# One order of 815 operations exchanged for another in a fused SSM and long-convolution kernel

## The chip, the cores and the metric

The kernel runs on one core of a Trainium2 chip. A core has five engines that run their own instruction queues side by side: TensorE (PE; its weight loads are shown apart, as PEld), VectorE (DVE), ScalarE (ACT), GpSimd (POOL) and SyncE (SP), which here only issues DMAs. They wait for each other by semaphores. PE writes its results into PSUM, which this kernel uses as 8 banks; DVE and ACT carry ("evict") them from there to SBUF. The metric is the device time of one execution in microseconds, the median of several runs.

## The reference

Two layers work on sequences of 2048 steps and 640 features; their outputs are put side by side. Setup and types are left out.

```python
def _A_ref(x, Lambda_re, Lambda_im, B_re, B_im, C_re, C_im, log_dt, Dskip):
    Lam_bar = exp(exp(log_dt) * Lam)
    B_bar = ((Lam_bar - 1.0) / Lam)[:, None] * Bmat
    Bu = einsum("bld,pd->blp", x, B_bar)
    for t in range(L):
        h = Lam_bar * h + Bu[:, t]          # 640 complex states
    return 2.0 * einsum("blp,dp->bld", hseq, Cmat).real + x * Dskip
...
def _B_ref(q, k, v, shift_k, ssm_k, ssm_D):
    k_shift = sum(k_pad[:, t:t + S] * shift_k[:, 3 - t] for t in range(4))
    kv = k_shift * v
    y = irfft(rfft(kv, 2 * S) * rfft(ssm_k, 2 * S))[:S]
    return q * (y + kv * ssm_D)
...
concatenate([a, b], axis=-1)
```

## The kernel before, in words

**One table sets everything.** The program is written as 815 operations. An operation is one step such as "these 20 matmuls" or "evict this PSUM group", with the memory that it reads and writes, from which its dependencies are found. A string, `ORDER` (behind line 1115), lists all of them: each entry has the operation's number, a letter for its engine (A = ACT, V = DVE, G = POOL, T = PE, t = PE in a narrow form of 64 output columns, S = SP) and a digit for its first PSUM bank. Line 1175 or so turns the string into a list, and `Program.emit` walks through it: each engine gets its operations in this order and runs them in this order, whatever else is ready. An operation waits for its dependencies, and the first one of a PSUM group also for the last holder of its banks. So the order decides what is queued behind a waiting instruction, the bank digit decides whose eviction a matmul waits for, and the letter decides what an eviction costs. Some operations have no instructions with some engines: where ACT evicts a group (a plain copy), a following operation multiplies or adds on DVE or POOL; where DVE evicts, it does both in one instruction, and the follower is empty.

**Part A (the SSM).** x is loaded transposed (L547), B_bar is built from the parameters (L517 and L512 load, L524 turns it). The base matmuls (L581) form Bu for blocks of 16 steps. Going up, neighbours are joined by multiplying with tables of powers of Lam_bar (four large tables, L457, multiplied on PE at L602; a fifth instruction at L457 is for part B); the groups are evicted at L598, L622 and L648. C is transformed with PE at L571 (evicted at L575). A scan over the 128 blocks (L679 to L690, all on DVE) reads its swapped input from a PSUM group at L679. Going down, L225 or L229 are the matmuls (a wide and a narrow form) and L728 (DVE) or L726 (ACT) the additions; the innermost level comes last. Sixteen output tiles follow: x is loaded (L736) into one of four buffers, multiplied with Dskip (L737; Dskip is loaded at L372), 20 matmuls (L225 or, narrow, 40 at L229), eviction on DVE (L754) or on ACT (L752) with an addition (L760) on POOL, and a store (L765). A load at L736 thus waits for the store, four tiles earlier, that read its buffer.

**Part B (the convolution).** k and v are loaded transposed (L814) in five slices, each convolved with four taps (products at L205 on DVE or L206 on ACT, sums at L840) and multiplied with v (L841), then written to DRAM (L847) and read back in another layout (L857). The transform goes in two stages per half of the features: L876 or L881 with evictions at L886, L900 with evictions at L913, both for the kernel ssm_k (loaded at L807) and for kv. The products in the frequency domain are five instructions per quarter (L924, two L927, L929, L931). Back it goes by L951 (evicted at L956) and L972, evicted on ACT (L988, then L995 multiplies with q) or on DVE (L990, with q at once); q is loaded at L825 in four pieces per half, and stored at L1006.

The names in the rows: `arena` is all of SBUF, `acc` all of PSUM, `kv_rows` the DRAM scratch.

## Time and profile before

| what | us |
|---|---|
| median of 3 runs | 188.28 (188.27 to 188.59) |
| span of the profiled execution | 187.3 |
| around the span, against that median | 0.98 |
| PE busy | 175.6 |
| DVE busy | 158.0 |
| ACT busy | 147.7 |
| POOL busy | 72.6 |

The profiled execution has no time of its own beside its span; the median of the runs stands in for it. A span is counted from the first to the last instruction on the engines. Busy times of one engine's instructions overlap slightly, since the next one starts before the last has left the pipeline. In all rows, an arrow in brackets names what ended the idle time before an instruction, and times are microseconds.

### The profile page before, as it was taken

How to read it: one execution, taken by the hardware profiler on the slowest of the kernel's cores; microseconds unless marked ns; L12 is line 12 of the kernel's file. 1: busy time of each engine (PE TensorE's matmuls, PEld its weight loads, DVE VectorE, ACT ScalarE, POOL GpSimd, SP SyncE). 2: the span in 40 equal slices, each digit the busy share in tenths (PEclk: the TensorE clock that was granted, in tenths of full speed). 3: DMA queues.
4: the chain of work that ended last, by engine and by line, in shares of the span. 5: the costliest groups of instructions: out<-in, count | busy, mean ns of one | idle time of the engine just before them, and what ended most of it. 6: DMA issues, size and time to landing. Idle time of an engine off the chain costs nothing.

```text
span 187.3 us, 7665 instructions
## 1 busy us (share of the span) xinstructions
PE 175.6 (94%) x3398; PEld 126.3 (67%) x3399; DVE 158.0 (84%) x225; ACT 147.7 (79%) x181; POOL 72.6 (39%) x68
## 2 busy tenths in 40 slices
PE   7998999999799979979997999999999999999992
PEld 2565666677468756656685688776588876887770
DVE  3537964679959899999969999899999999998961
ACT  2469699989899979999997997997898883985000
POOL 8679999900000000008803925730740000551620
PEclk9999999999999999999999999999999999999999
DMA  5999999799999989999989479402496993058996
GB/s 153 191 184 158 200 143 140 141 174 182 198 253 154 290 179 152 180 182 154 138 109 251 154 170 133 75 5 72 122 196 120 210 227 85 15 160 187 208 219 173
DMA packets 106682, 30.15 MB, mean 161 GB/s; under 512 B 101274, under 2 KB 106010, under 8 KB 106650
## 3 DMA queue, kind: packets, MB, share of 16 engines
q1 hardware_dynamic: 106332, 29.35, 86.7%
q8 instruction: 26, 0.43, 1.1%
q10 hardware_dynamic: 318, 0.33, 0.6%
q14 instruction: 6, 0.05, 0.1%
HBM read 11.32 MB, written 7.86 MB: 102 GB/s over the span
## 4 chain that ended last, share of the span: by engine, by line
PE 54%; DVE 23%; DMA 9%; ACT 8%; issue 3%; DVEq 0%; ACTq 0%
PE acc L225 17%; PE acc L581 13%; DMA arena<-in_B_k_dram 9%; PE acc L229 6%; DVE arena L728 6%; PE acc L900 6%; DVE arena L205 5%; ACT arena L913 5%; PE acc L951 4%; DVE arena L840 3%; PE acc L972 3%; PE acc L539 2%; DVE arena L754 2%; PE acc L881 1%; ACT arena L886 1%
## 5 line engine op out<-in xcount | busy, mean ns | idle before, releaser
L581 PE MATMUL acc<-arena 128*64 128x512 bf16 x400 | 45.6, 380 | 1.8 <-DVE arena L457 1.1
L913 ACT CAST arena<-acc 128x960 bf16<-128x960 f32 (+1 forms) x43 | 37.4, 916 | 4.0 <-PE acc L900 2.2
L225 PE MATMUL acc<-arena 128*128 128x320 bf16 (+2 forms) x255 | 36.4, 297 | 2.2 <-DVE arena L754 1.1
L581 PEld LDWEIGHTS <-arena 128*64 128x64 bf16 x400 | 26.0, 110 | 17.8 <-DVE arena L457 1.3
L886 ACT CAST arena<-acc 128x1024 bf16<-128x1024 f32 x37 | 35.8, 1034 | 2.1 <-PE acc L881 2.0
L225 PEld LDWEIGHTS <-arena 128*128 128x128 bf16 x256 | 23.7, 98 | 12.1 <-DVE arena L754 1.3
L841 POOL TENSOR_TENSOR arena<-arena 128x2048 bf16<-128x2048 bf16 x2 | 8.8, 4410 | 53.7 <-DVE arena L840 46.1
L900 PE MATMUL acc<-arena 128*64 128x160 bf16 x512 | 23.6, 235 | 1.8 <-DVE arena L679 1.4
L900 PEld LDWEIGHTS <-arena 128*64 128x64 bf16 x512 | 18.6, 110 | 8.3 <-ACT arena L913 2.2
L229 PE MATMUL acc<-arena 128*64 128x320 bf16 (+3 forms) x258 | 23.2, 313 | 0.5 <-DVE arena L690 0.5
L840 DVE TENSOR_TENSOR arena<-arena 128x2048 bf16<-128x2048 bf16 x14 | 17.6, 1256 | 4.5 <-ACT arena L206 4.3
L728 DVE TENSOR_TENSOR arena<-acc,arena 128x1024 bf16<-128x1024 f32 (+2 forms) x19 | 20.4, 1114 | 0.9 <-PE acc L229 0.5
L760 POOL TENSOR_TENSOR arena<-arena 128x640 bf16<-128x640 f32 x3 | 4.2, 1416 | 32.6 <-ACT arena L752 32.6
L956 ACT CAST arena<-acc 128x1024 bf16<-128x1024 f32 x16 | 15.4, 1025 | 1.7 <-PE acc L951 1.6
L229 PEld LDWEIGHTS <-arena 128*64 128x64 bf16 x258 | 13.0, 110 | 3.5 <-DVE arena L690 0.6
L876 PE MATMUL acc<-arena 128*64 128x128 bf16 x400 | 14.6, 220 | 0.2 <-ACT arena L886 0.2
L876 PEld LDWEIGHTS <-arena 128*64 128x64 bf16 x400 | 12.9, 110 | 2.4 <-ACT arena L886 0.9
L205 DVE TENSOR_SCALAR arena<-arena 128x2048 bf16<-128x2048 bf16 x15 | 11.0, 749 | 3.6 <-DMA arena<-in_B_k_dram 3.5
L754 DVE TENSOR_TENSOR arena<-acc,arena 128x640 bf16<-128x640 f32 x13 | 10.7, 820 | 3.5 <-PE acc L225 2.2
L206 ACT ACTIVATE arena<-arena 128x2048 bf16<-128x2048 bf16 (+2 forms) x10 | 11.1, 1112 | 1.5 <-DMA arena<-in_B_k_dram 1.5
L924 DVE TENSOR_TENSOR arena<-arena 128x2560 bf16<-128x2560 bf16 x8 | 11.9, 1484 | 0.1
L602 PE MATMUL acc<-arena 128*64 128x256 bf16 (+2 forms) x140 | 11.6, 291 | 0.1
(142 smaller groups left out, 284.4 us busy)
## 6 DMA issues: line engine op xcount, KB each, us to landing
out_dram<-arena SPq DMA_DIRECT2D x32, 160.0 KB, 3.3
arena<-in_B_ssm_k_dram SPq DMA_DIRECT2D x8, 320.0 KB, 6.1
kv_rows<-arena SPq DMA_DIRECT2D x5, 512.0 KB, 4.7
arena<-kv_rows SPq DMA_DIRECT2D x16, 160.0 KB, 4.0
arena<-in_A_x_dram SPq DMA_DIRECT2D x16, 160.0 KB, 3.5
arena<-in_B_q_dram SPq DMA_DIRECT2D x8, 320.0 KB, 6.3
arena<-in_A_B_im_dram ACTq DMA_DIRECT2D x1, 160.0 KB, 2.8
arena<-in_A_B_re_dram SPq DMA_DIRECT2D x1, 160.0 KB, 3.0
```

The lines of the kernel that those rows point to most:

```text
L205: vm = lambda e: lambda out, in_, by: e.tensor_scalar_mul(out=out, in0=in_, scalar1=by)
L225: e.matmul(out, lhsT=lhsT, rhs=rhs, start=start, stop=stop, skip_group_check=True)
L229: e.matmul(out[half], lhsT=lhsT[:, half], rhs=rhs, start=start, stop=stop, skip_group_check=True, tile_position=(0, 64 * r))
L581: e.matmul(o[64 * r:64 * r + 64], lhsT=self.BT[j][:, r, d, :], rhs=self.XP[:, d, 2 * q:2 * q + 2], start=(d == 0), stop=(d == 4), skip_gro ...
L728: e.tensor_tensor(out=o, in0=b, in1=o, op=ALU.add)
L754: e.tensor_tensor(out=two(ys), in0=two(B)[:, :, 0:320], in1=two(ys), op=ALU.add)
L840: P.add(f"ca{d}_{j}", tt, lambda e: e.tensor_tensor(out=t1, in0=t1, in1=t2, op=ALU.add), outs=[t1], ins=[t1, t2])
L876: e.matmul(B[64 * b:64 * b + 64, 128 * i:128 * i + 128], lhsT=lh[i], rhs=F[:, b, :], start=True, stop=True, tile_position=(0, 64 * b))
L886: P.add(f"e1{what}{hf}_{u}", {PACT: act(1024), PDVE: dve(1024)}, lambda e, B: c.CP[e](out=out, in_=(B.rearrange("p (l n s k) -> p k s l n" ...
L900: e.matmul(B[64 * s:64 * s + 64, 512 * b + 160 * i:512 * b + 160 * i + 160], lhsT=c.W[:, k, 64 * b:64 * b + 64], rhs=self.AS[hf][:, k, 160 ...
L913: c.CP[e](out=out, in_=b.rearrange("p r (k j n) -> p r k j n", k=n, j=4) if nj > 1 else b.rearrange("p r (k x) -> p r k x", k=n))
L956: P.add(f"er2{hf}_{u}", {PACT: act(1024), PDVE: dve(1024)}, lambda e, B: c.CP[e](out=out, in_=B.rearrange("p (s n b) -> p b s n", s=2, n=4 ...
```

## The change

Only the string changes. All operations and their dependencies stay, and all entries stand in another order. 57 operations change their engine, 8 matmul groups their form (the number of matmuls goes from 3399 to 3395), and 309 of the 418 operations that belong to a PSUM group get another bank.

```diff
 ORDER = (
-    "67G0 22V0 4T0 25V0 171T1 26G0 23V0 65V0 148G0 39V0 66V0 112G0 59V0 72G0 9T0 183S0 165T2 46G0 30G0 169T0 69G0 180S0 92T3 "
...
+    "148G0 18V0 125V0 19V0 65V0 23V0 20V0 13V0 182S0 9T4 39V0 66V0 69G0 92T5 8T6 93V5 171T7 94A0 95V0 37V0 72G0 122V0 10T0 102V0 22V0 "
...
```

From ACT to DVE go 19 operations: five evictions of part A's upward levels and of B_bar, five of L886 and L913, three conv taps, two small scalings, three evictions at L956 and L990, and the eviction of output tile 10 (L752 before, L754 now). From DVE to ACT go eleven: two upward evictions, two at L575, one L886, one small L728, three L956, one L990 and the eviction of output tile 15. From DVE to POOL go the one L457 of part B, an L929, an L931, four L737 and some followers; from POOL to DVE two L927, three L737 and some followers. Some loads change the queue between SP and ACT.

**First place: DVE around the fourth k slice.** The two L205 of the double row multiply the fourth k slice, as soon as it has landed, with its first two taps; L679, L682, L683 and L684 are the scan of part A's first half; the L457 ahead is part B's. Before:

```order
L666 COPY arena<-arena 128x1280
L841 TENSOR_TENSOR arena<-arena 128x2048
L457 TENSOR_TENSOR arena<-arena 128x1280
L682 TENSOR_TENSOR arena<-arena 128x640
L668 MEMSET arena 128x10
L205 TENSOR_SCALAR arena<-arena 128x2048 x2
L679 TENSOR_TENSOR arena<-acc,arena 128x640
L840 TENSOR_TENSOR arena<-arena 128x2048
L683 TENSOR_TENSOR arena<-arena 128x640
L205 TENSOR_SCALAR arena<-arena 128x2048
```

Now:

```order
L841 TENSOR_TENSOR arena<-arena 128x2048
L913 CAST arena<-acc 128x2x3x4x40
L679 TENSOR_TENSOR arena<-acc,arena 128x640
L682 TENSOR_TENSOR arena<-arena 128x640
L668 MEMSET arena 128x10
L683 TENSOR_TENSOR arena<-arena 128x640
L205 TENSOR_SCALAR arena<-arena 128x2048 x2
L684 SCALAR_TENSOR_TENSOR arena<-arena 128x640
L840 TENSOR_TENSOR arena<-arena 128x2048
L205 TENSOR_SCALAR arena<-arena 128x2048
```

L679, which stood behind the double L205, stands ahead of it, as do L682 and L683; in front of L679 there is now an eviction (L913). The L457 has gone to POOL. Further up, of part A's four tables (L457, numbers 0 to 3) before made 0 and 3 early, and 1 and 2 between the conv instructions of the second k slice. Now 0 and 1 come early, ahead of every conv instruction, and 2 and 3 as a double row directly ahead of the third k slice's first two L205.

**Second place: SP around the load of Dskip.** L814 are the transposing loads of k and v, L807 those of ssm_k's second half. Before:

```order
L814 DMA_TRANSPOSE arena<-in_B_v_dram 128x2048
L736 DMA arena<-in_A_x_dram 128x640
L814 DMA_TRANSPOSE arena<-in_B_k_dram 128x2048
L556 DMA_TRANSPOSE arena<-in_A_C_re_dram 128x1x640
L736 DMA arena<-in_A_x_dram 128x640
L807 DMA arena<-in_B_ssm_k_dram 32x80x64 x4
L372 DMA arena<-in_A_Dskip_dram 128x640
L736 DMA arena<-in_A_x_dram 128x640
```

Now:

```order
L814 DMA_TRANSPOSE arena<-in_B_v_dram 128x2048
L556 DMA_TRANSPOSE arena<-in_A_C_re_dram 128x1x640
L372 DMA arena<-in_A_Dskip_dram 128x640
L814 DMA_TRANSPOSE arena<-in_B_k_dram 128x2048
L807 DMA arena<-in_B_ssm_k_dram 32x80x64 x4
L736 DMA arena<-in_A_x_dram 128x640 x2
L814 DMA_TRANSPOSE arena<-in_B_v_dram 128x2048
```

The load of Dskip (L372), which stood behind the fifth k slice and four ssm_k pieces, stands ahead of both.

**Third place: SP around the last load of q.** L765 stores output tiles of part A, L736 loads an x tile into the buffer of such a store, L1006 stores part B. Before:

```order
L765 DMA out_dram<-arena 128x640
L825 DMA arena<-in_B_q_dram 32x32x160
L736 DMA arena<-in_A_x_dram 128x640
L825 DMA arena<-in_B_q_dram 32x32x160
L736 DMA arena<-in_A_x_dram 128x640
L765 DMA out_dram<-arena 128x640 x3
L736 DMA arena<-in_A_x_dram 128x640 x3
L1006 DMA out_dram<-arena 32x16x160 x4
```

Now:

```order
L765 DMA out_dram<-arena 128x640
L736 DMA arena<-in_A_x_dram 128x640
L765 DMA out_dram<-arena 128x640 x3
L736 DMA arena<-in_A_x_dram 128x640
L825 DMA arena<-in_B_q_dram 32x32x160
L736 DMA arena<-in_A_x_dram 128x640
L1006 DMA out_dram<-arena 32x16x160
L736 DMA arena<-in_A_x_dram 128x640
```

The last piece of q (L825) for the second half stood ahead of the three stores of tiles 9, 11 and 10; it now stands behind the three, which are in the order 10, 9, 11, and behind the L736 that loads into the buffer of tile 10.

**On PE**, at the last L728 of the innermost level, an L951 group of the first half now stands ahead of the L900 that needs the freed bank, where before it stood behind the output tile that follows. In the second half, an L951 group stands ahead of an L972 that it used to follow.

76 rows, old and new, of the table ORDER are left out of this document.

## The prediction

> **What bounds the kernel now.** I read the page first, for span and engine shares; then busy time by stage; then the chain of waits; then who waits for whom on TensorE (PE) and VectorE (DVE); last the timelines around the longest waits. The page and the windows:
>
> ```profile
> span 187.3 us, 7665 instructions
> PE 175.6 (94%) x3398; PEld 126.3 (67%) x3399; DVE 158.0 (84%) x225; ACT 147.7 (79%) x181; POOL 72.6 (39%) x68
> ...
> core 0: us, PE busy (x) PEld busy (x) DVE busy (x) ACT busy (x) POOL busy (x), PEclk, DMA share, GB/s
> 0.00:40.00 40.00, 38.37 (x343) 23.53 (x345) 25.18 (x69) 30.80 (x38) 34.03 (x51) 1.00 1.05 166
> 40.00:60.00 20.00, 18.76 (x301) 13.32 (x298) 16.89 (x23) 18.34 (x27) 0.00 (x0) 1.00 1.11 189
> 60.00:141.00 81.00, 76.04 (x1731) 56.23 (x1730) 76.94 (x89) 74.67 (x92) 28.76 (x11) 1.00 0.84 152
> 141.00:187.30 46.30, 42.38 (x1034) 33.18 (x1029) 39.01 (x47) 23.84 (x27) 9.79 (x6) 1.00 0.73 160
> ```
>
> The mean share of PE hides three regimes. Up to 40 us PE works on the base matmuls, DVE is loose and POOL builds tables. From 60 to 141 us DVE is busy 76.94 of 81.00 us and ACT 74.67: there is no room on either, and PE waits for them in small pieces. After 141 us ACT is half idle. The chain of waits shows which of these times counts (start, length, what):
>
> ```profile
> 41.15 1.42 DVE arena L205 x2
> ...
> 46.67 0.98 DVE arena L457
> ...
> 65.20 1.42 DVE arena L205 x2
> 66.62 0.74 DVE arena L679
> 67.41 0.61 PE acc L900 x12
> ...
> 135.91 1.24 DVE arena L728
> 137.19 1.93 PE acc L900 x48
> ...
> 161.68 5.47 PE acc L951 x160
> ...
> 169.98 1.70 PE acc L972 x176
> ```
>
> So there are two gates on DVE. **Gate 1** is the last L728 (the innermost level of A's downward scan), which ends at 135.91 + 1.24 = 137.15: it frees the PSUM bank that the next L900 needs, and from there PE runs on almost without a gap. **Gate 2** is the last product of part B, which ends at 159.82 + 1.68 = 161.5 and lets the second inverse stage (L951) begin:
>
> ```profile
> 159.82 1.68 DVE L931 TENSOR_TENSOR arena<-arena 128x1280 bf16<-128x1280 bf16 x2
> ```
>
> Between 41.15, where DVE gets the second k tile, and gate 1 lie 96.0 us that DVE must fill; its waits there are few:
>
> ```profile
> DVE arena L205 <- DMA arena<-in_B_k_dram: 3.5, 3, 1.9
> DVE arena L737 <- DMA arena<-in_A_Dskip_dram: 1.4, 1, 1.4
> ...
> 53.96 0.75 DVE L205 TENSOR_SCALAR arena<-arena 128x2048 bf16<-128x2048 bf16 x1 [1.90 <-DMA arena<-in_B_k_dram]
> ...
> 65.20 1.42 DVE L205 TENSOR_SCALAR arena<-arena 128x2048 bf16<-128x2048 bf16 x2 [0.65 <-DMA arena<-in_B_k_dram]
> ...
> 97.87 0.49 DVE L737 TENSOR_TENSOR arena<-arena 128x640 bf16<-128x640 bf16 x1 [1.38 <-DMA arena<-in_A_Dskip_dram]
> ```
>
> And two waits of PE for DVE are single long ones, both early:
>
> ```profile
> 48.12 2.35 PE L581 MATMUL acc<-arena 128*64 128x512 bf16 x20 [1.15 <-DVE arena L457]
> ...
> 67.41 0.61 PE L900 MATMUL acc<-arena 128*64 128x160 bf16 x12 [1.39 <-DVE arena L679]
> ```
>
> **The sum** is made against the profiled execution: span 187.3 us. The median of the runs shown is 188.28, that is 0.98 us around the span, which I keep.
>
> **What goes.** (1) Of the four tables at L457, before makes numbers 0 and 3 early and 1 and 2 between the conv instructions (L205, L840) of the second k slice, and PE waits 1.15 us for number 1. In the new order 0 and 1 come early, and 2 and 3 stand as a pair where DVE waited 1.90 us for the third k slice: the wait of PE goes, and that of DVE is filled. (2) L679 stood behind two L205 that wait for the fourth k slice; it now stands ahead of them, so the 1.39 us of PE go and the 0.65 us of DVE are covered by L679 and its neighbours. (3) The Dskip load stood in SP's queue behind big loads; it now stands ahead of the fifth k slice and of four ssm_k loads, and the 1.38 us should go. For DVE that is 1.90 + 0.65 + 1.38 = 3.93 us of waits.
>
> A new wait comes: the eviction L913 that stands just ahead of L679 waits for its matmuls on PE. No row shows it. Its bounds: nothing, if PE is ahead, up to the 1.39 us for which PE stood at that place; less than nothing is excluded, since a wait saves no work. I take 0.8, near the middle, since the wait and PE's own are two sides of one late pair.
>
> **What comes.** DVE gets more to do, by these groups of the page and of the view by shape:
>
> ```profile
> L886 DVE CAST arena<-acc 128x1024 bf16<-128x1024 f32 x3 | 3.6, 1215 | 0.0
> L913 DVE CAST arena<-acc 128x960 bf16<-128x960 f32 x3 | 3.5, 1154 | 0.0
> L927 DVE TENSOR_TENSOR arena<-arena 128x1280 bf16<-128x1280 bf16 x14 | 11.4, 819 | 0.1
> L929 POOL TENSOR_TENSOR arena<-arena 128x1280 bf16<-128x1280 bf16 x1 | 2.6, 2617 | 0.1
> L737 DVE TENSOR_TENSOR arena<-arena 128x640 bf16<-128x640 bf16 x11 | 7.4, 686 | 1.4 <-DMA arena<-in_A_Dskip_dram 1.4
> L575 DVE CAST arena<-acc 128x640 bf16<-128x640 f32 x4 | 3.3, 815 | 0.0
> L457 DVE TENSOR_TENSOR arena<-arena 128x1280 bf16<-128x1280 bf16 x5 | 8.2, 1652 | 0.0
> ```
>
> From 41.15 to the last product, DVE gains one L886 (1.22), three L913 (3.46), two L927 (1.64), two L737 (1.37) and small ones (one conv tap and one L648, together 1.2; three tiny scalings 0.4), 9.3 in all. It loses one L457 that goes to POOL (1.65), two L575 to ACT (1.63), an L929 and an L931 to POOL (1.64, at the 0.82 of an L927), three L737 (2.06, one of them only passes behind the last product) and small ones (0.9), 7.9 in all. Net **+1.4**. But the L931 and two of the lost L737 stood behind gate 1, so there these 2.2 us count as no loss, and DVE has 1.4 + 2.2, some 3.5 us, more to do ahead of it. Neighbouring DVE rows overlap (the chain counts 0.74 of an L679 that lasts 0.82), so 3.5 of durations are about 3.2 of time, and 1.4 are 1.3.
>
> Gate 1: +3.2 − 3.93 + 0.8 = **+0.1**. Unchanged, then; but one L951 group (16 of the 160 matmuls that last 5.47 us in the chain, 0.5 us) is now issued ahead of the L900 that waits there, so PE has 0.5 less left behind it: **−0.4** on the end.
> Gate 2: +1.3 − 3.93 + 0.8 = −1.8 if DVE alone set it. It can't get all of that, since the products take evictions of matmuls that come behind gate 1, and these come only 0.4 earlier. Ends −0.4 and −1.8; I take the middle, −1.1. An L972 group of 48 matmuls now stands behind this gate, where it stood ahead (48 of the 176 that last 1.70, so +0.4): **−0.7**.
>
> The later of the two decides, and they differ by less than I know them: I take **−0.6**. At the start, loads and weights trade places on SP and ACT's queue. PE's base matmuls run 38.37 of 40.00 us there, so a shift of a load can cost or bring up to the 1.63 that is left; I take nothing, for want of a row that leans either way. Evictions that pass from ACT to DVE cost a fifth more each (1215 ns against 1034):
>
> ```profile
> L886 ACT CAST arena<-acc 128x1024 bf16<-128x1024 f32 x37 | 35.8, 1034 | 2.1 <-PE acc L881 2.0
> ```
>
> That is inside the count above; what ACT is relieved of buys time only where ACT was late. Eight matmul groups change form: 4 instructions fewer, the L229 forms take about 0.3 us each: nothing.
>
> **A rule that speaks against it.** POOL gets the L457, an L929 and an L931 while DVE is full. Do they hinder each other? The trace has rows for both sides (duration in ns: least, median, most):
>
> ```profile
> L457 DVE TENSOR_TENSOR arena<-arena x5: 1481/1483/2326, 18.7 to 62.6; 128x1280 bf16<-128x1280 bf16 x5
> ...
> L737 DVE TENSOR_TENSOR arena<-arena x11: 481/484/1685, 97.9 to 175.0; 128x640 bf16<-128x640 bf16 x11
> ...
> 84.01 4.08 POOL L841 TENSOR_TENSOR arena<-arena 128x2048 bf16<-128x2048 bf16 x1 [46.12 <-DVE arena L840]
> 101.44 4.74 POOL L841 TENSOR_TENSOR arena<-arena 128x2048 bf16<-128x2048 bf16 x1 [7.61 <-DMA arena<-in_B_v_dram]
> ```
>
> So yes: now and then an instruction of DVE is longer by 0.84 or 1.20 us, or one of POOL by 0.66. The Trainium skill, page "SBUF — State Buffer", section "Who interferes with whom", has the reason: a DVE instruction with two SBUF inputs and a GpSimd instruction that reads SBUF share one port pair, and the one that comes second is blocked entirely. By that rule each POOL instruction added beside a full DVE may cost up to its own length, and one more of 2.6 us would make the sum +2.0 instead of −0.6. The trace agrees in kind, but the losses that it shows are fractions of a POOL instruction. My own count goes by the rows: in exchange for the three above and two L737, POOL gives up two L927 and two L737, one instruction more net; I count it at nothing, and one encounter more costs 0.84.
>
> **The rivals.**
> *The waits gone count in full.* DVE's extra work falls into gaps, both gates move by the waits alone, and PE gains 1.15 + 1.39: the end comes 1.8 (gate 2's lower end) to 2.5 earlier. Time about 186.3. For it: the chain does run through both waits. Against it: 76.94 busy of 81.00.
> *Nothing moves, or what is won is given back.* PE has 42.38 of 46.30 us behind 141 and the gates stay; or one more encounter of POOL and DVE takes 0.84 of the 0.6 won. Time 188.1 to 188.5. That the change doesn't do what it says is excluded as far as order goes: engines run their rows in order. But (3) may only hand the wait to the k load that Dskip now precedes.
> *DVE is overfull (slower).* The 3.2 us ahead of gate 1 aren't covered, because the waits of the three k loads are set by the transposes and recur at later instructions: then the gate moves +3.2 less a part, +1 to +2.5. Time 189.3 to 190.8.
> *The last q load comes late (slower).* This is the one I fear most. All L988 and L990 of the second half need four q loads (L825). Before, the last was issued long before its use:
>
> ```profile
> 150.62 1.27 SPq L825 DMA_DIRECT2D arena<-in_B_q_dram  x1
> ...
> SPq L736 <- DMA out_dram<-arena: 7.0, 5, 2.3
> ...
> L825 SPq DMA_DIRECT2D arena<-in_B_q_dram x8: 400/605/1693, 134.8 to 150.6; - x8
> ...
> DMA to landing us min/median/max: 4.2/6.3/7.6
> ```
>
> Now it stands on SP behind three stores of A's tiles and a load (L736) that waits until the first of these stores has landed. That store's tile is evicted on DVE behind all products, at about 161; it is waited for at most 2.3 us (the longest of the five waits above), then the load is issued, and q follows at about 164. Landing after 4.2 is 168.2, after the median 6.3 it is 170.3, after 7.6 171.6. In the chain of before the L972 ahead of these evictions begin at 169.98, and 176 of their matmuls last 1.70; in the new order 160 (1.55) precede the L225 that needs the bank of the first eviction, so with 0.6 won PE is there at 170.9. An eviction of 1.15 (as L913) stands between: PE stalls by what the landing exceeds 169.8, that is 0 to 1.8 us. Time 187.7 to 189.5, more if the issue itself slips. The deciding point is the landing at 169.8. Against it: fewer loads are under way then than at 144, so the landing should be nearer to 4.2 than to 7.6.
>
> **How the numbers follow.** The runs differ by 0.2% (188.27 to 188.59), about what a measurement of this kernel can tell from no change: faster means below 187.90, slower above 188.66. The forecast, −0.2 to −1.2 around **187.7**, gets 0.38; waits in full 0.10; nothing moves 0.21; DVE overfull 0.13; late q 0.18, of which 0.01 still ends faster and 0.01 within 0.2%. Of the forecast 0.02 falls within 0.2%. Faster 0.36 + 0.10 + 0.01 = 0.47, same 0.21 + 0.02 + 0.01 = 0.24, slower 0.13 + 0.16 = 0.29. The range leaves out the better half of the full waits and the worst of the two slower cases: 186.2 to 190.0. The forecast's own range is 187.1 to 188.1.
>
> **What would show it.** Right: no PE wait on L457 or L679 at 45 to 70 us over 0.5; no L737 wait on Dskip; the last L728 ending within 0.7 us of 137.15, the last L931 at about 160.4. Late q: a PE wait at an L225 near 171 on an L988 or L990, with L825 landing behind 169.8. Overfull: the last L728 ends behind 138. Wrong altogether: a wait of over 1 us at a place that none of these names, above all at the start, where the forecast has only a bound.

## The result, and the profile after

| what | before | after |
|---|---|---|
| median of the runs, one chip | 188.34 (188.27 to 188.59) | 196.25 (195.25 to 197.74) |
| ratio | | 1.0424 [1.0373, 1.0474] |
| span of the profiled execution | 187.3 | 194.6 |
| PE / DVE / ACT / POOL busy | 175.6 / 158.0 / 147.7 / 72.6 | 177.5 / 164.4 / 139.4 / 77.6 |

The change makes the kernel slower by 4.2%, some 8 us. Times and ratios here and below are those of the fast executions: one that took over 1.5% longer than the fastest of its kernel is left out. The profiled execution of after has a time of its own, 196.35, so 1.75 us lie around its span.

The page of after, and its busy time in the stretches that the prediction used (the last one ends later now):

```profile
span 194.6 us, 7661 instructions
...
PE 177.5 (91%) x3395; PEld 126.5 (65%) x3395; DVE 164.4 (85%) x231; ACT 139.4 (72%) x173; POOL 77.6 (40%) x70
...
0.00:40.00 40.00, 36.70 (x331) 21.55 (x333) 29.10 (x76) 24.70 (x34) 35.83 (x51) 1.00 1.09 165
40.00:60.00 20.00, 19.76 (x320) 13.28 (x317) 18.20 (x20) 17.56 (x22) 0.57 (x1) 1.00 1.10 218
60.00:141.00 81.00, 73.78 (x1644) 54.55 (x1640) 75.48 (x89) 69.21 (x89) 29.28 (x11) 0.98 0.88 145
141.00:194.60 53.60, 47.25 (x1116) 37.09 (x1112) 41.66 (x49) 27.90 (x32) 11.96 (x9) 0.99 0.63 140
```

Up to 40 us PE does 1.7 us less than before, and from 40 to 60 a full us more. Between 60 and 141 us it loses 2.3 us of busy time and 87 matmuls, and the granted clock is no longer 1.00. The waits say on whom (total, times, longest):

```profile
PE acc L900 <- DVE arena L728: 4.0, 3, 3.3
PE acc L581 <- DMA arena<-in_A_B_re_dram: 2.0, 1, 2.0
...
PE acc L225 <- ACT arena L988: 0.9, 1, 0.9
...
DVE arena L205 <- DMA arena<-in_B_k_dram: 3.2, 1, 3.2
...
ACT arena L988 <- DMA arena<-in_B_q_dram: 3.0, 1, 3.0
```

The waits on L457, L679 and Dskip are gone. In their place stands one long one: DVE waits 3.2 us for the fifth k slice, and PE 3.3 us for the L728 behind it. The timelines of DVE and PE show both, one behind the other:

```profile
90.80 1.42 DVE L205 TENSOR_SCALAR arena<-arena 128x2048 bf16<-128x2048 bf16 x2 [3.16 <-DMA arena<-in_B_k_dram]
92.14 3.81 DVE L728 TENSOR_TENSOR arena<-acc,arena 128x1024 bf16<-128x1024 f32 x4
96.75 1.16 DVE L913 CAST arena<-acc 128x960 bf16<-128x960 f32 x1 [0.81 <-PE acc L900]
...
93.41 0.61 PE L900 MATMUL acc<-arena 128*64 128x160 bf16 x12 [3.30 <-DVE arena L728]
```

Why does the fifth slice come late? All k slices use one buffer (`KT`; v has three), so a load may be issued only when the last tap has read the slice before it. The timeline of DVE around the third slice, in after:

```profile
48.86 1.23 DVE L841 TENSOR_TENSOR arena<-arena 128x2048 bf16<-128x2048 bf16 x1
50.01 1.22 DVE L886 CAST arena<-acc 128x1024 bf16<-128x1024 f32 x1
52.68 0.83 DVE L666 COPY arena<-arena 128x1280 f32<-128x1280 f32 x1 [1.46 <-PE acc L881]
53.42 2.88 DVE L457 TENSOR_TENSOR arena<-arena 128x1280 bf16<-128x1280 bf16 x2
56.23 1.41 DVE L205 TENSOR_SCALAR arena<-arena 128x2048 bf16<-128x2048 bf16 x2
...
61.18 0.75 DVE L205 TENSOR_SCALAR arena<-arena 128x2048 bf16<-128x2048 bf16 x1
...
63.23 1.23 DVE L841 TENSOR_TENSOR arena<-arena 128x2048 bf16<-128x2048 bf16 x1
64.59 1.16 DVE L913 CAST arena<-acc 128x960 bf16<-128x960 f32 x1
```

With L841 DVE is through with the second slice, at 48.86 + 1.23 = 50.09 (before: 1.90 ahead of 53.96, so 52.06). Yet the third slice's taps start at 56.23, where they started at 53.96 before. In front of them stand not only the two tables, but an eviction (L886) and a copy (L666) that itself waits 1.46 us for PE. The last tap ends at 61.18 + 0.75 = 61.93. SP's issues in the timeline of before, from the fourth k slice to the fifth:

```profile
59.81 3.06 SPq L814 DMA_TRANSPOSE arena<-in_B_k_dram  x1
...
74.64 2.93 SPq L814 DMA_TRANSPOSE arena<-in_B_v_dram  x1
...
78.25 2.16 SPq L814 DMA_TRANSPOSE arena<-in_B_k_dram  x1
```

And in that of after:

```profile
61.96 2.23 SPq L814 DMA_TRANSPOSE arena<-in_B_k_dram  x1
...
77.07 3.34 SPq L814 DMA_TRANSPOSE arena<-in_B_v_dram  x1
80.46 2.05 SPq L556 DMA_TRANSPOSE arena<-in_A_C_re_dram  x1
82.56 0.58 SPq L372 DMA_DIRECT2D arena<-in_A_Dskip_dram  x1
83.24 3.79 SPq L814 DMA_TRANSPOSE arena<-in_B_k_dram  x1
```

The fourth slice's load goes out 0.03 us behind that tap, 2.15 us later than before; in a_r16k4, below, it also follows by 0.03. SP issues one load after the other, and v comes 2.4 us late too. Then C and Dskip, which stand ahead of the fifth k slice now, take 2.8 us more, and that slice is issued 5.0 us later than before.

The end of after, by its chain of waits (start, length, what), shows the last q load:

```profile
167.84 3.52 DMA out_dram<-arena
...
171.75 5.40 DMA arena<-in_B_q_dram
...
177.26 0.70 ACT arena L988
...
178.00 5.61 PE acc L225 x40
```

It is issued behind the store that L736 waits for, lands at 177.15, and the eviction behind it holds PE for 0.9 us.

### The profile page after: what moved, and what is told of

Same layout as the page of the kernel before. It is cut to its first block, busy times and chain, and to the rows that moved or that the text cites. A ratio compares the mean times of both kernels' runs of the same rounds, so it can differ in the third digit from the quotient of the medians.

```text
span 194.6 us, 7661 instructions
## 1 busy us (share of the span) xinstructions
PE 177.5 (91%) x3395; PEld 126.5 (65%) x3395; DVE 164.4 (85%) x231; ACT 139.4 (72%) x173; POOL 77.6 (40%) x70
## 4 chain that ended last, share of the span: by engine, by line
PE 39%; DVE 18%; DMA 17%; SPq 12%; ACT 8%; issue 4%; DVEq 0%; ACTq 0%
PE acc L581 16%; PE acc L225 7%; DVE arena L728 5%; PE acc L229 5%; DMA out_dram<-arena 4%; SPq L807 4%; DMA arena<-in_A_B_re_dram 4%; SPq L547 4%; PE acc L602 3%; PE acc L900 3%; DVE arena L754 3%; DMA arena<-in_B_q_dram 3%; PE acc L876 2%; ACT arena L913 2%; DMA arena<-in_B_v_dram 2%
## 5 line engine op out<-in xcount | busy, mean ns | idle before, releaser
L913 ACT CAST arena<-acc 128x960 bf16<-128x960 f32 (+1 forms) x40 | 35.2, 896 | 9.9 <-PE acc L900 9.5
L225 PE MATMUL acc<-arena 128*128 128x320 bf16 (+3 forms) x262 | 38.0, 299 | 1.3 <-ACT arena L988 0.9
L886 ACT CAST arena<-acc 128x1024 bf16<-128x1024 f32 x36 | 34.9, 1032 | 3.3 <-PE acc L876 1.5
L225 PEld LDWEIGHTS <-arena 128*128 128x128 bf16 x262 | 24.2, 98 | 11.2 <-ACT arena L988 1.0
L900 PE MATMUL acc<-arena 128*64 128x160 bf16 x512 | 24.3, 243 | 4.3 <-DVE arena L728 4.0
L900 PEld LDWEIGHTS <-arena 128*64 128x64 bf16 x512 | 20.1, 115 | 9.4 <-DVE arena L728 5.6
L229 PE MATMUL acc<-arena 128*64 128x320 bf16 (+3 forms) x248 | 22.1, 310 | 1.3 <-DVE arena L690 0.6
L728 DVE TENSOR_TENSOR arena<-acc,arena 128x1024 bf16<-128x1024 f32 (+2 forms) x18 | 20.0, 1154 | 0.3 <-PE acc L229 0.2
L841 POOL TENSOR_TENSOR arena<-arena 128x2048 bf16<-128x2048 bf16 x2 | 8.3, 4164 | 26.6 <-DMA arena<-in_B_v_dram 17.5
L205 DVE TENSOR_SCALAR arena<-arena 128x2048 bf16<-128x2048 bf16 (+1 forms) x20 | 14.7, 752 | 3.4 <-DMA arena<-in_B_k_dram 3.2
L956 ACT CAST arena<-acc 128x1024 bf16<-128x1024 f32 x17 | 16.3, 1027 | 1.3 <-PE acc L951 1.3
L754 DVE TENSOR_TENSOR arena<-acc,arena 128x640 bf16<-128x640 f32 x13 | 10.7, 822 | 3.9 <-PE acc L225 2.8
L927 DVE TENSOR_TENSOR arena<-arena 128x1280 bf16<-128x1280 bf16 x16 | 12.6, 819 | 0.2
L309 POOL TENSOR_TENSOR arena<-arena 128x512 int32<-128x512 int32 x8 | 12.3, 1546 | 0.7 <-DVE arena L435 0.6
L457 POOL TENSOR_TENSOR arena<-arena 128x1280 bf16<-128x1280 bf16 x1 | 3.1, 3147 | 22.9 <-ACT arena L648 22.9
```

The source lines that it names most:

```text
L205: vm = lambda e: lambda out, in_, by: e.tensor_scalar_mul(out=out, in0=in_, scalar1=by)
L225: e.matmul(out, lhsT=lhsT, rhs=rhs, start=start, stop=stop, skip_group_check=True)
L229: e.matmul(out[half], lhsT=lhsT[:, half], rhs=rhs, start=start, stop=stop, skip_group_check=True, tile_position=(0, 64 * r))
L728: e.tensor_tensor(out=o, in0=b, in1=o, op=ALU.add)
L754: e.tensor_tensor(out=two(ys), in0=two(B)[:, :, 0:320], in1=two(ys), op=ALU.add)
L886: P.add(f"e1{what}{hf}_{u}", {PACT: act(1024), PDVE: dve(1024)}, lambda e, B: c.CP[e](out=out, in_=(B.rearrange("p (l n s k) -> p k s l n" ...
```

## The experiments

Ratios are against runs of before on the same chip, with their 95% intervals. Before took 186.6 to 187.6 us there.

### Single suspects of after

**a_ctl** is after once more, on another chip: 194.67, ratio 1.0427 [1.0367, 1.0487]. The loss doesn't hang on the chip.

> The changed kernel itself, as the yardstick for the three runs beside it on the same chip: 1.042 times before, within the 1.0373 to 1.0474 measured.

**a_k4tap** moves the fifth slice's load ahead of the fourth v slice's, and, as the one buffer then demands, the fourth slice's last tap forward on DVE:

```diff
 DVE
 L840 TENSOR_TENSOR arena<-arena 128x2048
+L205 TENSOR_SCALAR arena<-arena 128x2048
 L679 TENSOR_TENSOR arena<-acc,arena 128x640
...
 L684 SCALAR_TENSOR_TENSOR arena<-arena 128x640
-L205 TENSOR_SCALAR arena<-arena 128x2048
 SP
+L814 DMA_TRANSPOSE arena<-in_B_k_dram 128x2048
 L814 DMA_TRANSPOSE arena<-in_B_v_dram 128x2048
 L556 DMA_TRANSPOSE arena<-in_A_C_re_dram 128x1x640
 L372 DMA arena<-in_A_Dskip_dram 128x640
-L814 DMA_TRANSPOSE arena<-in_B_k_dram 128x2048
```

> The changed kernel, with the last tap of the fourth k slice (L205) put back on DVE directly behind that slice's third sum, and the load of the fifth k slice (L814) put on SP ahead of the fourth v slice, of C and of Dskip. Theory 'late k slice' (the fifth slice lands at 90.7 instead of 84.2, DVE waits 3.2 us for it and PE 3.3 behind that): the slice lands before 86, both waits go, and the time falls by 3.3 to 4.4 us, to 192.0 to 193.0. Theory 'DVE overfull' (the wait only stands where DVE would be late anyway): it falls by less than 1.5 us, to 195 or more.

Measured: 193.50, ratio 1.0318 [1.0256, 1.0381]. DVE no longer waits for k, and PE's wait falls from 3.30 to 1.72 us, not to nothing: the v slice, later now, brings a POOL product beside the two taps, which take 3.07 us instead of 1.42 (DVE's and POOL's timelines):

```profile
88.07 3.07 DVE L205 TENSOR_SCALAR arena<-arena 128x2048 bf16<-128x2048 bf16 x2
...
85.86 4.07 POOL L841 TENSOR_TENSOR arena<-arena 128x2048 bf16<-128x2048 bf16 x1 [19.32 <-DMA arena<-in_B_v_dram]
```

So the k wait is worth about 1% of the 4.2, by point values whose intervals just overlap.

**a_k4first** puts the fifth slice's load directly behind the fourth v slice, ahead of C and Dskip, and moves nothing on DVE. **a_k4q** does the same and brings the last q load ahead, as a_q below.

```diff
 L814 DMA_TRANSPOSE arena<-in_B_v_dram 128x2048
+L814 DMA_TRANSPOSE arena<-in_B_k_dram 128x2048
 L556 DMA_TRANSPOSE arena<-in_A_C_re_dram 128x1x640
 L372 DMA arena<-in_A_Dskip_dram 128x640
-L814 DMA_TRANSPOSE arena<-in_B_k_dram 128x2048
```

> The changed kernel with the load of the fifth k slice on SP directly behind the fourth v slice, ahead of C and Dskip; nothing else is moved, DVE keeps its order. In the run that put k ahead of v and the tap back, DVE's wait for k was gone, but the two L205 took 3.07 us instead of 1.42, since the v slice came later and POOL's L841 fell beside them. Theory 'late k slice, and the port': here v is not delayed, L841 on POOL is over by 88.3, k lands at about 87, L205 takes 1.4 to 2.0, and 3.0 to 3.6 us are won against the changed kernel. Theory 'DVE overfull': under 1.5.

> The same and also the last load of q ahead of the three stores. Theory 'late q': 0.9 to 1.3 us less than the kernel with the k slice alone. Rival: the same within 0.4.

Measured: 194.07, ratio 1.0389 [1.0329, 1.0449], and 193.30, 1.0350 [1.0293, 1.0406]. The k wait is gone, but now C is late, and PE waits for it (a_k4first):

```profile
PE acc L571 <- DMA arena<-in_A_C_re_dram: 2.2, 1, 2.2
```

What stands in this queue is a closed sum: with everything 2.2 us late, one load or another is waited for, whichever comes last.

**a_start** gives the start loads before's order. It came out at 204.12, ratio 1.0865 [1.0797, 1.0932], and tells nothing of the start: the load of shift_k fell behind the transposes, and its cast on ACT, with the evictions behind it, waited 9.45 us.

> The changed kernel with the loads at the start (B, parameters, x, B transposed, shift_k, first k slice) in the order and on the queues of before. Theory 'start': the second B transpose lands at 18.5 instead of 19.9, the base matmuls go on 1.3 us earlier, and this stays to the end: about 195.0. Rival 'absorbed': at 60 us the changed kernel's PE has the same lost time as before's (the lag of 1.35 is made up by then), so the k slices and DVE set the time from there and the end moves by less than 0.4: 195.9 to 196.3.

**a_start2** avoids that: shift_k's load goes behind the B transposes, and its cast (L796) behind the evictions on ACT.

```diff
 SP
-L547 DMA_TRANSPOSE arena<-in_A_x_dram 128x5x256 x2
-L790 DMA arena<-in_B_shift_k_dram 128x5x4
-L547 DMA_TRANSPOSE arena<-in_A_x_dram 128x5x256 x2
+L547 DMA_TRANSPOSE arena<-in_A_x_dram 128x5x256 x4
 L512 DMA_TRANSPOSE arena<-in_A_B_im_dram 128x5x384
 L512 DMA_TRANSPOSE arena<-in_A_B_re_dram 128x5x384
+L790 DMA arena<-in_B_shift_k_dram 128x5x4
```

> The changed kernel with the load of shift_k behind the two B transposes on SP, as before had it, and the small cast that reads it (L796, on ACT) moved to just ahead of the first tap, since it made all of ACT wait for this load in the first try. Theory 'start': the second B transpose lands 0.6 to 1.4 earlier and the end comes as much earlier. Rival 'absorbed': the end moves by less than 0.4, because the k slices and DVE set the pace from 45 us on.

Measured: 194.14, ratio 1.0410 [1.0334, 1.0486] beside 1.0427 for a_ctl. PE's wait for B is 0.8 us; with after's start it is 2.0 in after and 1.1 in a_ctl, so the edit takes away 0.3 to 1.2. The end shows nothing of it that can be told from noise, and the intervals are too wide to exclude such an amount.

**a_q** issues the last q load ahead of the three stores:

```diff
 L736 DMA arena<-in_A_x_dram 128x640
+L825 DMA arena<-in_B_q_dram 32x32x160
 L765 DMA out_dram<-arena 128x640 x3
-L736 DMA arena<-in_A_x_dram 128x640
-L825 DMA arena<-in_B_q_dram 32x32x160
-L736 DMA arena<-in_A_x_dram 128x640
+L736 DMA arena<-in_A_x_dram 128x640 x2
```

> The changed kernel with the last load of q (L825) of the second half put on SP ahead of the three stores of tiles 10, 9 and 11. Theory 'late q': ACT's wait of 3.0 us for q at L988 and PE's of 0.9 behind it go, the end comes 0.9 to 1.7 earlier: 194.5 to 195.4. Rival: the output tiles and stores behind it set the end, less than 0.4 is won: 195.9 or more.

Measured: 194.36, ratio 1.0323 [1.0235, 1.0412]. ACT's wait for q is gone. Between a_k4first and a_k4q the same edit takes 0.4%; both pairs of intervals overlap, so q is worth something between nothing and 1%.

### Single suspects put into before

**b_k4late** changes before alone: the fifth slice's load goes behind C, one ssm_k piece and Dskip, which itself comes ahead of the three other pieces.

```diff
 L736 DMA arena<-in_A_x_dram 128x640
-L814 DMA_TRANSPOSE arena<-in_B_k_dram 128x2048
 L556 DMA_TRANSPOSE arena<-in_A_C_re_dram 128x1x640
 L736 DMA arena<-in_A_x_dram 128x640
-L807 DMA arena<-in_B_ssm_k_dram 32x80x64 x4
+L807 DMA arena<-in_B_ssm_k_dram 32x80x64
 L372 DMA arena<-in_A_Dskip_dram 128x640
+L814 DMA_TRANSPOSE arena<-in_B_k_dram 128x2048
+L807 DMA arena<-in_B_ssm_k_dram 32x80x64 x3
```

> The kernel before with one thing moved: the load of the fifth k slice stands on SP behind the last piece of C, one x tile, one piece of ssm_k and Dskip, so that it is issued at about 84 instead of 78.3 and lands at about 90.5 instead of 84.2. DVE reaches its first tap at 88.2 in before. Theory 'late k slice': DVE waits 2 to 3 us there and all of it shows at the end: 190.3 to 191.5. Theory 'DVE overfull': before has slack for it, less than 0.6 is lost: under 188.9.

Measured: 189.71, ratio 1.0113 [1.0055, 1.0172], so +2.1 us. The trace has the pair of waits that after has:

```profile
PE acc L229 <- DVE arena L728: 2.7, 1, 2.7
...
DVE arena L205 <- DMA arena<-in_B_k_dram: 4.7, 2, 2.8
```

A fifth slice that is late by itself costs 2.1 us, somewhat less than the 2.7 that PE then waits. The edit also takes away DVE's wait of 1.38 us for Dskip, so it isn't the late load alone.

**b_gain** puts two early steps of the change into before: tables 0 and 1 come early instead of 0 and 3, and the scan goes ahead of the fourth slice's taps. The two other tables stay between the taps of the second slice.

```diff
 L668 MEMSET arena 128x10
+L679 TENSOR_TENSOR arena<-acc,arena 128x640
+L683 TENSOR_TENSOR arena<-arena 128x640
 L205 TENSOR_SCALAR arena<-arena 128x2048 x2
-L679 TENSOR_TENSOR arena<-acc,arena 128x640
-L840 TENSOR_TENSOR arena<-arena 128x2048
-L683 TENSOR_TENSOR arena<-arena 128x640
+L840 TENSOR_TENSOR arena<-arena 128x2048
```

> The kernel before with only the two steps of the change that the prediction counted as gains: tables 0 and 1 of L457 early and 2 and 3 late, and the first L679 with its L687 ahead of the two L205 of the fourth k slice. PE's waits of 1.15 and 1.39 us go. Theory 'they count at the end': 0.6 to 2.0 us less than before. Theory 'absorbed' (PE then only waits for DVE sooner; in the changed kernel PE was 1.3 us ahead of before at 66 us and level again at 77): within 0.4 us of before.

Measured: 187.45, ratio 1.0019 [0.9996, 1.0042]. PE's wait of 1.15 us on L457 is gone from the trace, that on L679 is 0.7 us instead of 1.39, and the end doesn't move. DVE's waits don't go: it still waits for the third slice, and where it waited 0.65 us for the fourth, L679 now waits 1.36 for matmuls.

```profile
51.98 0.76 DVE L205 TENSOR_SCALAR arena<-arena 128x2048 bf16<-128x2048 bf16 x1 [1.95 <-DMA arena<-in_B_k_dram]
```

**b_tap** delays the third slice's last tap in before by one L457 (1.4 us), and so the load of the fourth slice:

```diff
 L840 TENSOR_TENSOR arena<-arena 128x2048
+L457 TENSOR_TENSOR arena<-arena 128x1280
 L205 TENSOR_SCALAR arena<-arena 128x2048
...
 L841 TENSOR_TENSOR arena<-arena 128x2048
-L457 TENSOR_TENSOR arena<-arena 128x1280
```

> The kernel before with one DVE instruction moved the other way: part B's L457 (1.48 us) goes from behind the third k slice's product to ahead of that slice's last tap. DVE does the same work; the last tap ends 1.4 later, at 61.0, the fourth slice is issued at 61.2 instead of 59.8, and DVE's wait for it grows from 0.65 to about 2. Theory 'the tap frees the load': 0.6 to 1.6 us slower, ratio 1.003 to 1.009. Rival 'before has slack there': within 0.4 us.

Measured: 188.05, ratio 1.0025 [0.9988, 1.0063], that is between 0.2 us faster and 1.2 slower. The fourth slice's load goes out 6.9 us behind the third slice's first tap instead of 5.9, and 0.02 us behind its last one, but DVE waits only 0.85 us for it instead of 0.65. So a late tap costs before little, if anything; the interval doesn't decide between the two theories. In after the late tap and the longer queue ahead of the fifth slice come together.

### The late tap in after

**a_r16** moves one DVE copy, nothing else: L666 from ahead of the two tables to behind the third slice's last sum. **a_r16b** is the same on another chip. **a_r16k4** adds the edit of a_k4first, **a_four** those of a_q and a_start2 as well.

```diff
 L886 CAST arena<-acc 128x64x2x8
-L666 COPY arena<-arena 128x1280
 L457 TENSOR_TENSOR arena<-arena 128x1280 x2
 L205 TENSOR_SCALAR arena<-arena 128x2048 x2
...
 L840 TENSOR_TENSOR arena<-arena 128x2048
+L666 COPY arena<-arena 128x1280
```

> The changed kernel with one DVE instruction moved: L666 (a copy into the buffer of ssm_k's first half, which waits 1.5 us for the last L881) goes from ahead of the two L457 to behind the third k slice's last sum. Theory 'the tap frees the load': there is one k buffer, so the taps of the third slice, which start at 56.2 in the changed kernel and at 54.0 in before, hold back the load of the fourth (issued at 62.0 instead of 59.8) and with it all that SP issues afterwards. With the copy behind them the taps start at 54.0 to 54.3, the fourth slice is issued at 59.8 and the fifth at about 81 instead of 83.2; DVE's wait for the fifth falls from 3.2 to about 1 and the time by 2.0 to 2.6 us against the changed kernel (ratio to before about 1.030). Rival 'only the late order counts' (SP's own order from 77 us on): the fifth slice stays at 83, less than 0.6 is won.

> The changed kernel with the copy at L666 behind the third k slice's last sum, once more, for a trace of it. Expected: ratio to before 1.016 to 1.026 as measured; the fourth k slice is issued at about 59.8, the fifth at about 81 and lands by 88.5; DVE waits under 1.2 for it, PE under 1 at the L900 behind.

> The same and the fifth k slice's load directly behind the fourth v slice, ahead of C and Dskip. Alone, that move won only 0.3% (C came late in its place, and PE waited 2.2 us for it at L571). Theory 'the tap frees the load': with SP 2.2 us earlier both come in time, no wait for k or C over 0.5; 3.3 to 4.2 us less than the changed kernel (ratio about 1.022). Rival 'DVE overfull': the L728 behind come no earlier than 1 us before the changed kernel's, ratio 1.032 or more.

> The same, and also the last load of q ahead of the three stores, and shift_k's load behind the B transposes with its cast (L796) moved behind ACT's second eviction. If the four causes add up: another 0.9 for q and 0.6 to 1.3 for the start, ratio about 1.012; what is left over before is then what DVE's added work ahead of the last L728 costs (0.6 to 1 us from 128 to 140 us, 0.8 at 157 to 167).

| kernel | us | ratio |
|---|---|---|
| a_r16 | 190.71 | 1.0210 [1.0157, 1.0263] |
| a_r16b | 192.01 | 1.0237 [1.0167, 1.0308] |
| a_r16k4 | 191.90 | 1.0254 [1.0194, 1.0314] |
| a_four | 191.51 | 1.0227 [1.0169, 1.0285] |

One copy of 0.8 us, put 8 us later, takes half of the loss away: from 4.2 to 2.1 or 2.4%. That is 3.4 to 4 us, more than the 2.0 to 2.6 expected; the granted clock of a_r16 is 1.00, and that of after 0.98 to 0.99 (the last section shows what that costs). The trace of a_r16k4 shows the chain set right (DVE, then SP, then DVE):

```profile
53.76 1.42 DVE L205 TENSOR_SCALAR arena<-arena 128x2048 bf16<-128x2048 bf16 x2
...
59.50 2.95 SPq L814 DMA_TRANSPOSE arena<-in_B_k_dram  x1
...
80.42 1.93 SPq L814 DMA_TRANSPOSE arena<-in_B_k_dram  x1
...
87.33 1.42 DVE L205 TENSOR_SCALAR arena<-arena 128x2048 bf16<-128x2048 bf16 x2
```

The third slice's taps start at 53.76 (before: 53.96), the fourth slice is issued at 59.50 (59.81), and the fifth slice's taps start at 87.33 without a wait. (This kernel also has the fifth load ahead of C and Dskip; it goes out at 80.42, 0.02 us behind the fourth slice's last tap.) With before's order they start at 88.22 in before and at 86.94 in h_ba (below), so no loss is left there. DVE itself is hardly earlier than in after: the L913 ahead of L679 starts at 64.35 (64.59 in after), and DVE is ready for the fifth slice at 87.3 in a_r16k4 and at 87.64 in after, where it then waits 3.16 us. So the copy acts through the load rather than through DVE's own time. In the trace of a_r16b, which has the copy alone and runs 4 us late by the end of the second slice (L841 at 52.78, 48.62 in a_r16k4), the fourth load follows its tap by 0.04 us as well, DVE has no wait for the fifth slice, and PE none over 0.3 for L728. The orders of SP and of q that the other two kernels add bring nothing more that can be measured.

**a_r16act** takes a_r16 and gives ACT back six of the operations that the change moved to DVE: one L886, three L913, one L648 and one tap. **a_r16all** adds before's order of the loads behind the fourth v slice (k, C, the four ssm_k pieces, Dskip).

```diff
 DVE
-L886 CAST arena<-acc 128x64x2x8
...
-L913 CAST arena<-acc 128x2x3x4x40
...
-L648 CAST arena<-acc 128x256
...
-L205 TENSOR_SCALAR arena<-arena 128x2048
...
-L913 CAST arena<-acc 128x2x3x4x40 x2
+L913 CAST arena<-acc 128x2x3x4x40
...
-L728 TENSOR_TENSOR arena<-acc,arena 128x4x256 x4
-L913 CAST arena<-acc 128x2x3x160
-L728 TENSOR_TENSOR arena<-acc,arena 128x4x256
+L728 TENSOR_TENSOR arena<-acc,arena 128x4x256 x5
```

> The same, and six of the operations that the change gave to DVE are back on ACT (one L886, three L913, one L648, one L206): DVE has 5.8 us less to do between 41 and 138 us, ACT 6.7 more. Theory 'DVE overfull' for the rest: 1.2 to 2.5 us less than with the copy alone, ratio 1.010 to 1.014. Rival 'the loads set the pace' (k, C and ssm_k behind one another on SP): within 0.6 us of the copy alone.

> The same, and the loads behind the fourth v slice in the order of before: fifth k slice, C, four pieces of ssm_k, Dskip. If both theories hold, 0.5 to 1.5 less than the run before it, ratio 1.003 to 1.010; if the load order is a closed sum (whoever is last is waited for), no better than it within 0.6 us.

Measured: 194.35, ratio 1.0371 [1.0307, 1.0434], and 199.36, 1.0642 [1.0578, 1.0706]. Both are slower than a_r16. In a_r16act PE waits 2.6 us at L881 and L900 for ACT's L913 (0.3 in a_r16k4), and ACT waits 3.2 us for q:

```profile
PE acc L881 <- ACT arena L913: 1.3, 1, 1.3
PE acc L900 <- ACT arena L913: 1.3, 3, 0.5
```

In a_r16all DVE's L737 waits 3.1 us for Dskip. So these six can't simply be handed back at their places. That the order around them is fitted to their engines is my reading.

### The two halves

**h_ba** takes before's order for the first 460 entries, up to about 98 us, and after's for the rest; **h_ab** the other way round.

```python
h_ba = before[:460] + [e for e in after if e not in before[:460]]
h_ab = after[:459] + [e for e in before if e not in after[:459]]
```

> Before's order, engines and banks for the first 460 entries (to about 98 us, the last tap of the fifth k slice), then the changed kernel's for the rest. By the lost time of PE in the two traces, 2.9 us of the 7.3 arise behind that cut (0.6 to 1.0 at 128 to 140 us, 0.8 at 157 to 167, about 1 at the q wait). Theory 'two halves': ratio 1.010 to 1.018. Rival 'all from the first half' (the second half's waits only follow from its lateness): within 0.4% of before.

> The changed kernel's order for its first 459 entries (to the same place), then before's for the rest. Theory 'two halves': ratio 1.020 to 1.030, and with the run beside it the sum is 0.036 to 0.048. Rival 'all from the first half': 1.038 or more. If lateness is made up in before's second half: under 1.015.

Measured: 190.85, ratio 1.0180 [1.0136, 1.0223], and 192.91, 1.0284 [1.0236, 1.0332]. The losses add up to 4.6%, about the 4.2 of after. So the first half, with the late k chain in it, isn't all. Where the second half loses shows when each trace is divided at the gates: start of the fifth slice's taps, end of the L728 behind which the chain of waits goes on with L900 (gate 1), end of the last L931 (gate 2), start of the last L225, end of the span. The L728 of gate 1 is the fourth of five: in before's chain it ends at 137.15, and the fifth, the last, at 138.27. In the new order an L913 stands between the two. The rows of h_ba that carry this:

```profile
86.94 1.41 DVE L205 TENSOR_SCALAR arena<-arena 128x2048 bf16<-128x2048 bf16 x2
...
131.78 4.78 DVE L728 TENSOR_TENSOR arena<-acc,arena 128x1024 bf16<-128x1024 f32 x4
136.61 1.16 DVE L913 CAST arena<-acc 128x960 bf16<-128x960 f32 x1
137.76 1.23 DVE L728 TENSOR_TENSOR arena<-acc,arena 128x1024 bf16<-128x1024 f32 x1
...
160.13 0.82 DVE L931 TENSOR_TENSOR arena<-arena 128x1280 bf16<-128x1280 bf16 x1
...
178.19 5.61 PE L225 MATMUL acc<-arena 128*128 128x320 bf16 x40
```

The same of after:

```profile
136.54 4.78 DVE L728 TENSOR_TENSOR arena<-acc,arena 128x1024 bf16<-128x1024 f32 x4
...
165.64 0.82 DVE L931 TENSOR_TENSOR arena<-arena 128x1280 bf16<-128x1280 bf16 x1
...
184.53 5.61 PE L225 MATMUL acc<-arena 128*128 128x320 bf16 x40
```

The stretches between these points, worked out in the same way for seven traces (us; gate 1 by the chain):

| second half | kernel | taps to gate 1 | gate 1 to gate 2 | gate 2 to last L225 | last L225 to end |
|---|---|---|---|---|---|
| old | before | 48.93 | 24.35 | 16.50 | 9.30 |
| old | b_gain | 48.23 | 24.36 | 16.49 | 9.15 |
| old | h_ab | 50.04 | 24.37 | 16.48 | 9.10 |
| new | h_ba | 49.63 | 24.38 | 17.24 | 9.91 |
| new | a_r16k4 | 50.98 | 24.36 | 17.14 | 9.89 |
| new | a_four | 51.52 | 24.37 | 17.13 | 10.08 |
| new | after | 50.54 | 25.12 | 18.07 | 10.07 |

But for the first column, and for after with its waits, the kernels with the same second half agree within 0.2 us. Up to gate 1 h_ba takes 0.7 to 1.4 us longer than the two with before's order throughout, h_ab 1.1 to 1.8 (its first 9 us still have the new order), and those with the new order in both halves 1.6 to 3.3. From gate 1 to gate 2 the new order neither wins nor loses. It loses 0.65 to 0.75 until the last L225 (1.6 in after, with the q wait of 0.9 in it), and 0.6 to 0.9 behind it, where three stores at L765 stand at the end of SP's queue instead of two. In h_ba that makes 0.7 to 1.4 + 0.75 + 0.6 or 0.75 = 2.1 to 2.9 us; timed were 2.5 to 4.2.

No kernel was faster than before.

## Why the prediction was wrong

**The step that failed** is (1) under what goes: "the wait of PE goes, and that of DVE is filled". PE's wait did go, and so did DVE's. But I counted as filling only the pair of tables. The order puts L886 and the copy L666 there too, and L666 brings a wait of its own for PE, for which the sum has no term: DVE came 1.97 us earlier to this place, without the tables ahead of it, and then spent 6.14 us (50.09 to 56.23) where before it spent 1.90: 2.88 on the tables, 2.05 on L886 and L666, 1.46 on the wait, less some overlap. I treated the landings of k as given times at which DVE may be late without harm, and even the slower rival had them "set by the transposes". In fact DVE sets the fourth slice's, since its last tap frees the one buffer for the next load, and SP's queue hands the delay on; the loads that now stand ahead of the fifth slice add to it. a_r16 shows it: that copy alone makes half of the loss. In after's trace the late fifth slice costs PE's wait of 3.30 us and the half clock that follows (below), an estimated 1.7 us more.

In the terms of the sum, the work was sized well and the waits were not. From the second slice's taps to gate 1 DVE is busy 89.72 of 96.00 us in before (41.15 to 137.15) and 91.94 of 99.28 in after (42.06 to 141.34). That is 2.2 us more work, and 3.4 with the L913 that now stands ahead of the last L728, where I counted 3.5. But DVE is idle 1.1 us longer, where the sum has 3.93 − 0.8 = 3.1 less.

**The gains** in (1) and (2) were given a price at the end. b_gain has the two waits of PE gone or halved, and ends at 1.0019 [0.9996, 1.0042]: nothing of them shows there. It doesn't have DVE's two waits filled. In after and a_r16k4 these are gone, but others stand in their place: 1.46 us for L666 in the one, 1.69 us for ACT ahead of L913 in the other. So the 2.55 us that I subtracted for them at both gates weren't won; whether they could have paid at the end without such a new wait, no run shows.

**(3)** came out as an aside of mine had it, "may only hand the wait to the k load that Dskip now precedes": L737 waits no more, and L205 waits 3.16.

**The new wait on L913** was taken as 0.8, ahead of L679. None came there: that L913 starts at 64.59, 0.13 us behind the end of the L841 ahead of it. The wait of 0.81 us in after is that of another L913, at 96.75, behind PE's late L900.

**Gate 1 and gate 2** were to stay (+0.1) and to come 1.1 us earlier. They came 4.2 (137.15 to 141.34) and 5.0 us (161.50 to 166.46) later. What I called the last L728 is the fourth of five; the last ends at 138.27 in before and, behind the L913, at 143.76 in after. The L951 group that is issued ahead of the waiting L900 was to save 0.4 us; between the gates nothing of it is seen, 24.35 to 24.38 us with either order. The stage to gate 1 is longer in h_ba by 0.7 to 1.4 us, with DVE busy 47.63 of 49.63 us there and 45.80 of 48.93 in before: that agrees in kind with **DVE is overfull**. It isn't shown to be the cause: a_r16act, in which DVE has less to do there (46.77 us, 48.40 in a_r16k4), still takes 51.4 (50.98). Which of the exchanged engines in the second half costs these 0.7 to 1.4 us stays open.

**The end** was mis-sized. I booked +0.4 for matmuls that pass behind gate 2; all kernels with the new end lose 1.25 to 1.6 us there without the q wait, half of it behind the last matmul, for which the sum has no term. No run changes the end alone, so the stores as its cause are read from traces only.

**Late q** was the rival I feared most, with a landing from 168.2 to 171.6 and 0 to 1.8 us of stall. It landed at 177.15, 5.5 us behind the latest of these, 5.0 of which are the delay of gate 2, and PE waited 0.9. The mechanism was right, and it is the small part.

**The start**: my "nothing" within 1.63 isn't contradicted, and it isn't shown either. PE waits 2.0 us for B and goes on at 20.00, where before it went on at 18.65. That is 1.35 us, in the range that I gave. a_start2, in which PE goes on at 19.08 (19.59 in a_ctl), ends within 0.2% of a_ctl, with intervals of 0.6 to 0.8% on either side.

**The signs**: a wait of over 1 us "above all at the start" was to show that the forecast is wrong altogether, and the 2.0 us for B are one.

**The port rule**: an encounter more was to cost 0.84. In after no instruction of DVE beside one of POOL's is longer by more than 0.11 us (an L682) from 41 to 170 us; nearly all that ran beside them there read PSUM (L728, L754, L913). POOL's own L457 took 3.15 us instead of the 2.6 assumed.

**Span and time**: later profiled executions, of both orders, lie 1.7 to 1.9 us around their span. By that the one of before took some 189.1, and the 0.98 that I added was 0.8 too small. It changes nothing in the difference: 7.3 us between the spans and 0.8 make the 8 of the medians.

## What to carry to other kernels

Where a single buffer is loaded again and again, the load's time isn't given: follow it back to the last reader, and count every instruction and every wait ahead of that reader, then what stands behind the load in its queue. A wait that is taken away ahead of such a chain needn't pay for anything behind it. Two orders can be divided at one point and crossed; if the losses add up, each half can be looked into by itself, and a table of the stretches between fixed points shows where. Take these points from the chain of waits: the last L728 is a poor one, since the new order moves an L913 across it, and with it 1.2 us from one stretch to the other.

## What the runs showed of the hardware that wasn't expected

**A wait of PE can cost more than its length.** The windows of after, right behind the wait of 3.30 us (the first number behind POOL's busy time is the granted clock):

```profile
92.00:94.00 2.00, 0.59 (x14) 0.56 (x16) 2.00 (x4) 0.00 (x0) 1.64 (x1) 1.00 1.20 152
94.00:96.00 2.00, 2.00 (x28) 1.09 (x24) 1.94 (x2) 1.73 (x3) 2.00 (x1) 0.57 1.23 124
96.00:98.00 2.00, 2.00 (x38) 2.00 (x36) 1.25 (x2) 1.09 (x2) 0.42 (x1) 0.58 1.10 131
98.00:100.00 2.00, 2.00 (x46) 1.81 (x42) 2.00 (x3) 1.53 (x3) 0.00 (x0) 1.00 0.60 154
```

From 94 to 98 us PE is busy all the time at a clock of 0.57. In windows of 1 us it is 0.64, 0.50, 0.50 and 0.65: some 3.4 us at half speed, which loses an estimated (1 − 0.575) × 4 = 1.7 us. The same dip stands behind waits of 3.73 us (a_q, where it lasts twice as long), 2.62 (a_ctl), and 2.24 and 2.20 (a_k4q, a_k4first); none behind 2.10 (h_ab), 1.98 (a_start2) and 1.72 (a_k4tap), and none behind 2.71 in b_k4late. Nor is 2.2 us a bound: in a_r16b one stands behind the wait of 2.00 us for B at the start (0.72 from 20 to 22 us, 0.50 from 22 to 24), and after has none behind its 2.01 at the same place. So the length alone doesn't decide. The Trainium skill, page "TensorE: Matmul & The Clock Gate", section "What's actually happening", has the clock halved after an idle window of about 3.4 us, and full again after as long a busy time. The dips of 3.4 us agree, and so does a_q's of twice that; that a wait of 2.0 us was enough, and one of 2.7 wasn't, the traces show beside it.

**A product of POOL can double a tap of DVE**: the two L205 of a_k4tap took 3.07 us beside L841 on POOL, and 1.42 in before, after and a_r16k4. The Trainium skill, page "SBUF — State Buffer", section "Who interferes with whom", says that such an instruction can contend with one of GpSimd for a shared port pair, and that the one that comes second then waits for the other's end. The trace agrees, with the overlap as the measure: L841 had begun at 85.86 and ran on for 1.86 us behind the start of the taps at 88.07, and 1.65 us were lost. So it is in before's rows too: the L841 at 101.44 lost 0.66 us, and DVE's L924, begun at 100.77, ran on for 0.81 beside it.
